# A Mamba-2 scan in front of a cosine router: another order of the scan's steps, with banks of their own for the last outputs

## The chip, the cores and the metric

The kernel runs on one core of one Trainium2 chip. The metric is the device time of one execution in microseconds (us), lower is better. A profiled execution comes with its span (first to last instruction of the core), the granted clock of TensorE and the instructions of all engines: PE (TensorE matmul), PEld (its weight loads), DVE (VectorE), ACT (ScalarE), POOL (GpSimd) and SP (SyncE, which issues loads here).

## What is computed

Two blocks follow each other: a state-space scan over 4 batches, 8 heads and 768 tokens, and a top-1 mixture of 8 experts over the 3072 tokens that come out of it.

```python
for c in range(nc):                       # chunks of 32 tokens, nc = 24
    cum = np.cumsum(la, axis=-1)          # la = log of the decays a
    L = np.exp(cum[:, :, :, None] - cum[:, :, None, :]) * causal
    y_intra = einsum('bhij,bhjd->bhid', einsum('bhin,bhjn->bhij', Cc, Bc) * L, xc)
    y_inter = einsum('bhin,bhnd->bhid', Cc, state) * exp(cum)[..., None]
    y[:, :, sl] = y_intra + y_inter
    state = exp(sum(la))[..., None, None] * state + sum over j of B_j x_j * exp(cum_last - cum_j)
...
logits = xn @ en.T / tau                  # x = y as 3072 tokens of 256
expert_idx = argmax(logits, axis=1)
...
out[mask] = gate_w[mask, None] * (np.maximum(x[mask] @ w1[e], 0.0) @ w2[e])   # for each expert e
```

## The kernel before

The kernel takes chunks of 128 tokens (`Q`), each in two halves of 64 (`HQ`). There are 6 such chunks (`NC`) and 4 batches, and one step of the scan treats a pair of batches of one chunk, so there are 12 pairs (`NP`), two to a chunk. The order of the instructions on every engine is the order in which the Python code calls the functions, and nothing reorders them. Each engine works its own list in order and waits where an operand isn't there.

`begin` (L1358) loads the first data, keeps TensorE busy with products of zeros (L1377, 15 of them with 512 columns), turns the decays into factors and does the parts of pair 0 that need no state. `scan` (L1450) then runs steps s = 1 to 11. A step is made of:

- `inner` (L393, matmuls at L401): the products of C and B of pair s into `pg`. `causal` (L408) masks them on DVE into `g`.
- `from_states` (L427; L437 for the first half with `Tp`, L442 for the second with `Tq`) and `within` (L448; L458): the outputs of pair s-1 from the carried states and from the pair's own tokens, both into the bank pair `py`. `keep_outputs` (L555; L558) copies them on ACT to `yT`.
- `sums` (L465; L473): what pair s adds to the states, into columns 256 to 383 of `pg`. `states` (L480) folds it into the carried states, on ACT, DVE and POOL; `blocks_of_first` and `blocks_of_second` lay them out as `Tq` and `Tp` for `from_states`.
- `finish` (L563; L567): the outputs `yT` of pair s-2 are turned so that tokens lie on partitions, and the logits come with them, into `pz`. `keep_tokens` (L573; L577) copies them on ACT to `yt`, and `keep_rows` (L580) writes them to DRAM by a DMA that ACT issues.
- `scale_x` (POOL, `xs`), `scale_c` (POOL, `cp`) and `split_c` (ACT, `cm`) prepare the next pairs.

The routing of a chunk is spread over the steps: `pick` and `picked` (DVE) find each token's expert, `count` (POOL) counts them, `ranks` (L623; L631, ten small bf16 instructions on PE) numbers them, `hots` and `rows_hot` (DVE, and POOL for `Z`) make one-hot matrices, and `tables` (L680; L683) and `add_table` place the token numbers in a table by expert. `scan_end` (L1526) finishes pair 11 and the last two chunks' routing, while expert job J0, which takes tokens of the first four chunks, starts: a gather of its rows by POOL (`early`, L1605), `turn`, then `plain_up` (L1042) and `plain_down` (L1053). `moe` (L1613) does the rest of the experts.

Loads go through SP's queue in order. The table `LOADS` (L1424) says what is loaded in which of four places of a step; each load waits (`behind`, L338) for the last matmul issued so far.

Of PE's program, one fp32 matmul is two weight loads and two products, so four instructions; one in bf16 is two.

Of the kernel before, what the change touches and what calls it, by code (L numbers as in the profile page):

```python
# [124 lines left out]
def more_route_consts(k):  # L125
    nc = k.nc
    k.before = tile_(k, "before", [128, 128], BF16)
    k.ones = tile_(k, "ones", [128, 128], BF16)
# [297 lines left out]

def from_states(k, p):  # L427
    nc = k.nc
    c, b, t = pair(k, p)
    s = k.un[p]  # L430
    for i in range(2):
        first = c > 0 and i == 0
        a = slice(128 * i, 128 * i + 128)
        if c > 0:
            for g in range(2):
                r = slice(64 * g, 64 * g + 64)
                nc.tensor.matmul(  # L437
                    k.py[r, 0, a], lhsT=k.Tq[2 * c][r, b + i].rearrange("p q d -> p (q d)"),
                    rhs=s.cm[r, i, 0].rearrange("p v s -> p (v s)"), start=first, stop=False,
                    tile_position=(64 * g, 64 * g), skip_group_check=True,  # L440
                )
        k.last = nc.tensor.matmul(  # L442
            k.py[:, 1, a], lhsT=k.Tq[2 * c + 1][:, b + i].rearrange("p q d -> p (q d)"),
            rhs=s.cm[:, i, 1].rearrange("p v s -> p (v s)"), start=first, stop=(c == 0), skip_group_check=True,
# [3 lines left out]
def within(k, p):  # L448
    nc = k.nc
    c, b, t = pair(k, p)  # L450
    s = k.un[p]
    for i in range(2):
        for v in range(2):
            for q in range(4):
                for h in range(2):
# [3 lines left out]
                        k.py[r, h, a : a + HQ], lhsT=s.xs[m, i, n : n + 32], rhs=s.g[m, q, 2 * i + v, :],  # L459
# [5 lines left out]
def sums(k, p):  # L465
# [14 lines left out]
def states(k, p):  # L480
# [21 lines left out]
    if not last:  # L502
# [3 lines left out]
        )  # L506
    blocks_of_first(k, i, bb, u[0])
# [47 lines left out]
def keep_outputs(k, p):  # L555
# [3 lines left out]
        out=s.yT[:].rearrange("p j h s -> p h j s"), in_=k.py[:, :, 0:256].rearrange("p h (j s) -> p h j s", j=4)  # L559
    )  # L560


def finish(k, p):  # L563
    yT = k.un[p].yT
    for i in range(2):
        for j, at in ((0, 0), (1, LG)):
            k.last = k.nc.tensor.matmul(  # L567
                k.pz[:, i, at : at + Y1], lhsT=yT[:, 2 * i + j].rearrange("p h s -> p (h s)"), rhs=k.turn[:, j, :],
# [4 lines left out]
def keep_tokens(k, p):  # L573
# [3 lines left out]
    k.nc.scalar.copy(out=k.yt[c][:, b : b + 2, :], in_=k.pz[:, :, 0:W])  # L577
# [12 lines left out]
def pick(k, c):  # L590
# [9 lines left out]
    n = w.tile(ub, F32, name="nth", tag="nth")  # L600
# [35 lines left out]
def hots(k, c, at):  # L636

    nc = k.nc
    w = k.work
# [15 lines left out]
    k.hot[c] = r, ge  # L655


def rows_hot(k, c):
# [699 lines left out]
def begin(k):  # L1358
# [11 lines left out]
    load(k, 0, ("ct", "bt", "x", "b"))  # L1370
    expert_emb(k)
# [4 lines left out]
    for i in range(15):  # L1376
        nc.tensor.matmul(k.pg[:, 3, :], lhsT=k.zero[:, 0:128], rhs=k.zero[:], start=True, stop=True)  # L1377
    decays(k, 0)
    centre_decays(k, 0)
# [10 lines left out]
    behind(k, load(k, 1, ("ct",)), k.last)  # L1390
    load_decays(k, (4, 5), (nc.sync,))
# [10 lines left out]
    behind(k, load(k, 1, ("bt",)), k.last)  # L1402
# [5 lines left out]
    behind(k, load(k, 1, ("x0",)), k.last)  # L1408
    warm(k, 3)
# [350 lines left out]
```

## Time and profile before

| what | us |
|---|---|
| three runs, median (lowest, highest) | 273.12 (272.39, 273.99) |
| the profiled execution's own time | 271.15 |
| its span, first to last instruction | 269.2 |
| PE busy in the span | 249.0 (92%) |
| DVE, ACT, POOL busy | 172.2, 122.3, 130.4 |
| mean granted clock of TensorE | 0.936 of full |

In the rows of the trace, a time is counted from the span's start. A row of the timeline has the start, the duration, the engine, the line, the tile written and those read, the count, and in brackets the idle time of the engine just before, with what ended it; "issue" means that nothing which the profile shows was waited for. Matmuls of one group overlap, so the distance from one group's start to the next group's is what a group costs, not the duration of its row.

### The profile page before, as it was taken

To read this page: it belongs to the slowest core of one execution; us is meant where nothing else is said; L and a number is where in the kernel's file an instruction comes from. 1 tells how busy PE (TensorE), PEld (TensorE's weight loads), DVE (VectorE), ACT (ScalarE), POOL (GpSimd) and SP (SyncE) were. 2 spreads that over 40 slices of the span, in tenths; PEclk is the share of its full clock that TensorE was granted. 3 is DMA by queue.
4 is the path that set the end of the run, shared out by engine and by line. 5 is a ranking of instruction groups with operands and counts; after the bars stand their busy time and mean duration, and the time that the engine had idled before them with its cause. 6 is when DMAs were issued, how large, how long until landed. Compare 5 with 4: busy or idle time off the path is not lost.

```text
span 269.2 us, 7547 instructions
## 1 busy us (share of the span) xinstructions
PE 249.0 (92%) x2921; PEld 222.7 (83%) x2922; DVE 172.2 (64%) x502; ACT 122.3 (45%) x342; POOL 130.4 (48%) x242
## 2 busy tenths in 40 slices
PE   8879989999888998999999999999999999999790
PEld 2657758787667998999999999999899899899670
DVE  7757763766522480639839869948947957948630
ACT  3354562554212235456337535717626627626520
POOL 8773967466242273830635445455365365305214
PEclk9977995999955799999999999999999999999997
DMA  5586858745412069990534525526525121001001
GB/s 170 171 238 202 273 120 253 230 129 161 136 59 83 1 196 317 376 258 18 189 100 139 184 67 191 172 65 201 173 68 189 29 64 39 20 0 49 11 0 53
DMA packets 22949, 36.32 MB, mean 135 GB/s; under 512 B 2601, under 2 KB 15282, under 8 KB 22912
## 3 DMA queue, kind: packets, MB, share of 16 engines
q1 hardware_dynamic: 16272, 25.78, 30.7%
q0 software_dynamic: 3024, 6.67, 8.8%
q10 hardware_dynamic: 3616, 3.39, 3.7%
q8 instruction: 23, 0.38, 0.6%
q14 instruction: 14, 0.11, 0.1%
HBM read 29.33 MB, written 6.52 MB: 133 GB/s over the span
## 4 chain that ended last, share of the span: by engine, by line
PE 72%; issue 13%; ACT 5%; DMA 3%; POOL 3%; DVE 1%; POOLq 1%; ACTq 0%
PE by L927 10%; PE bx L927 9%; PE bx L987 9%; PE pz L567 6%; PE by L987 5%; PE py L458 4%; DMA out_dram<-yof,s_rest 3%; PE py L442 3%; PE bx L1042 3%; PE pg L401 3%; PE py L437 2%; PE by L1042 2%; PE bx L1053 2%; ACT sqf L863 2%; PE pg L1377 2%
## 5 line engine op out<-in xcount | busy, mean ns | idle before, releaser
L1026 POOL DMA_INDIRECT out_dram<-yof,s_rest x28 | 28.8, 1028 | 46.3 <-ACT yof L1025 45.0
L851 POOL DMA_INDIRECT xgf<-rows,g_rest x28 | 31.9, 1139 | 8.0 <-issue 7.8
L867 POOL TENSOR_TENSOR nrf<-nrf,half 104x4 f32<-104x4 f32 x7 | 7.3, 1041 | 31.0 <-ACT sqf L863 27.3
L567 PE MATMUL pz<-turn,yT 128*128 128x136 f32 x96 | 18.2, 343 | 1.1 <-ACT yt L577 0.6
L411 DVE TENSOR_TENSOR g<-pg,mask 128x1024 f32<-128x1024 f32 x12 | 14.7, 1221 | 4.2 <-PE pg L401 4.0
L567 PEld LDWEIGHTS pz<-turn,yT 128*128 128x128 f32 x96 | 15.6, 238 | 2.0 <-issue 1.0
L558 ACT COPY yT<-py 128x512 f32<-128x512 f32 x12 | 7.0, 583 | 16.5 <-PE py L458 15.0
L577 ACT COPY yt<-pz 128x528 f32<-128x528 f32 x12 | 7.2, 598 | 16.1 <-PE pz L567 16.1
L386 POOL TENSOR_TENSOR xs<-x,rT 128x512 f32<-128x512 f32 x12 | 12.7, 1062 | 3.2 <-DMA x<-in_x_dram 1.5
L524 POOL TENSOR_TENSOR T<-u,whole 128x64 f32<-128x64 f32 x22 | 7.6, 349 | 13.3 <-DVE u L499 12.7
L458 PE MATMUL py<-g,xs 64*32 64x64 f32 x768 | 12.3, 245 | 0.8 <-issue 0.6
L863 ACT ACTIVATE sqf<-xgf 104x256 f32<-104x256 f32 x28 | 11.6, 415 | 1.7 <-DVE h12f L974 1.0
L927 PE MATMUL by<-xsf,w 128*128 128x208 f32 (+6 forms) x56 | 11.8, 333 | 0.6 <-DVE h22f L956 0.6
L442 PE MATMUL py<-cm,Tq 128*128 128x128 f32 x48 | 12.3, 348 | 0.0
L952 DVE TENSOR_TENSOR h12f<-bx,cf 128x416 f32<-128x416 f32 (+6 forms) x7 | 3.9, 555 | 12.9 <-ACT yof L1025 8.6
L401 PE MATMUL pg<-cm,bt 32*64 32x128 f32 x384 | 10.0, 306 | 2.1 <-issue 1.5
L927 PE MATMUL bx<-xsf,w 128*128 128x208 f32 (+6 forms) x56 | 11.7, 331 | 0.0
L458 PEld LDWEIGHTS py<-g,xs 64*32 64x32 f32 x768 | 9.5, 116 | 2.5 <-issue 1.9
L927 PE MATMUL bx<-xsf,s 128*128 128x208 f32 (+6 forms) x56 | 11.4, 326 | 0.0
L927 PE MATMUL by<-xsf,s 128*128 128x208 f32 (+6 forms) x56 | 11.4, 326 | 0.0
L927 PE MATMUL by<-xTf,w 128*128 128x208 f32 (+6 forms) x56 | 11.4, 326 | 0.0
L927 PE MATMUL bx<-xTf,w 128*128 128x208 f32 (+6 forms) x56 | 11.4, 326 | 0.0
(330 smaller groups left out, 702.9 us busy)
## 6 DMA issues: line engine op xcount, KB each, us to landing
w<-in_moe_w_dram SPq DMA_DIRECT2D x14, 1024.0 KB, 4.9
rows<-yt ACTq DMA_DIRECT2D x12, 264.0 KB, 2.2
x<-in_x_dram SPq DMA_DIRECT2D x10, 256.0 KB, 4.2
w<-in_moe_w_dram SPq DMA_DIRECT2D x8, 256.0 KB, 3.1
ct<-in_CT_dram SPq DMA_DIRECT2D x6, 256.0 KB, 2.8
bt<-in_BT_dram SPq DMA_DIRECT2D x6, 256.0 KB
b<-in_B_dram SPq DMA_DIRECT2D x6, 256.0 KB, 5.6
F<-fd SPq DMA_DIRECT2D x4, 260.0 KB
```

The costliest lines, as they stand in the source:

```text
L386: k.nc.gpsimd.tensor_tensor(out=s.xs[:].rearrange("p i (h d) -> p (i h) d", d=D), in0=t.x[:, b : b + 2, :].rearrange("p i (h d) -> p (i h) ...
L401: k.last = nc.tensor.matmul(k.pg[m, q, 128 * i : 128 * i + 128], lhsT=t.bt[r, b + i, m], rhs=s.cm[r, i, h].rearrange("p v s -> p (v s)"), ...
L411: k.nc.vector.tensor_tensor(out=s.g[:], in0=k.pg[:, :, 0:256].rearrange("p q (t i) -> p q t i", t=4), in1=k.mask[:].unsqueeze(1).unsqueeze ...
L442: k.last = nc.tensor.matmul(k.py[:, 1, a], lhsT=k.Tq[2 * c + 1][:, b + i].rearrange("p q d -> p (q d)"), rhs=s.cm[:, i, 1].rearrange("p v ...
L458: k.last = nc.tensor.matmul(k.py[r, h, a : a + HQ], lhsT=s.xs[m, i, n : n + 32], rhs=s.g[m, q, 2 * i + v, :], start=(c == 0 and i == 0 and ...
L567: k.last = k.nc.tensor.matmul(k.pz[:, i, at : at + Y1], lhsT=yT[:, 2 * i + j].rearrange("p h s -> p (h s)"), rhs=k.turn[:, j, :], start=(j ...
L851: k.nc.gpsimd.indirect_dma_start(out=s.x[:, i, 0:W], out_offset=None, in_=k.rows[0:rows, :], in_offset=bass.IndirectOffsetOnAxis(ap=s.g_id ...
L863: nc.scalar.activation(sq[:], s.x[:, i, :].rearrange("p (j w) -> p j w", j=KD)[:, :, 0:128], ACT.Square, accum_out=s.nr[:, i : i + 1],)
L927: s.k.nc.tensor.matmul(bank[:, w * i : w * i + w], lhsT=a[:, 2 * g + i, :], rhs=s.r1[p], start=(p in (1, 2, 5) and i == 0), stop=True, ski ...
L987: s.k.nc.tensor.matmul(bank[:, 0:w], lhsT=a[:, g, :], rhs=r[:, g, 0:w], start=(p in (1, 2, 5) and g == 0), stop=True, skip_group_check=True,)
L1026: d = nc.gpsimd.indirect_dma_start(out=k.out[:, :], out_offset=bass.IndirectOffsetOnAxis(ap=s.s_idx[0:n, i : i + 1], axis=0), in_=y[0:n], ...
L1042: nc.tensor.matmul(bank[:, 0:n], lhsT=s.wt.w1[:, j, 128 * f : 128 * f + 128], rhs=s.xT[:, j, 0:n], start=(j == 0), stop=(j == KD - 1),)
```

## The change

The scan is written in another order. Steps 1 and 2 go to a function of their own, `first_steps`; `scan` runs steps 3 to 11.

- Within a step, `finish` of pair s-2 and its `keep_tokens` stand right behind `inner`, then `ranks`, then `sums` and `states` of pair s; `from_states` and `within` of pair s-1, with `keep_outputs`, come last. Before, `from_states` and `within` stood behind `inner`, and `finish` was last.
- `from_states` does the four blocks of `Tp` for both batches, then the two of `Tq`; before, the two kinds took turns.
- The places of a chunk's tokens are found a step sooner: `ranks` runs at even steps with pair-wise functions split up (`pick1`, `pick2`, `hots1`, `hots2`, `columns_hot`), and `ranks` writes `py` instead of `pz`.
- The outputs of the last pair (11) go to columns of `pg`, and its tokens to `py`; the table of chunk 3 and J0's gather come in step 11, before `causal`.
- The sums of the last chunk leave out the half that no later chunk reads.
- `begin` loads `ct` and `bt` of chunk 1 at once; `LOADS` has three places in a step, not four.
- The products of zeros are 80 with 64 columns in place of 15 with 512, and 8 with 128 columns in place of 3 with 512 ahead of step 1.
- `scan_end`: two DMAs of rows become one, `plain_up` 2 stands ahead of `ranks` of chunk 5, `plain_up` 4 ahead of the last `tables`.

On PE, an odd step with a table (s = 7 in the list after; before, the table stood in even steps, here s = 8). L401 is `inner`, L437 and L442 `from_states`, L458 `within`, L473 `sums`, L683 `tables`, L567 `finish`. Before:

```order
L401 MATMUL pg<-cm,bt 64x128 x16
L437 MATMUL py<-cm,Tp 64x128 x2
L442 MATMUL py<-cm,Tq 128x128
L437 MATMUL py<-cm,Tp 64x128 x2
L442 MATMUL py<-cm,Tq 128x128
L458 MATMUL py<-g,xs 32x64 x32
L473 MATMUL pg<-xs,b 32x64 x16
L683 MATMUL pz<-Z,A 104x32 x4
L567 MATMUL pz<-turn,yT 128x136 x4
```

After; the lines of the changed file are L579 for `finish`, L479 for `sums`, L440 and L446 for `from_states`, L712 for `tables` and L464 for `within`:

```order
L401 MATMUL pg<-cm,bt 64x128 x16
L579 MATMUL pz<-turn,yT 128x136 x4
L479 MATMUL pg<-xs,b 32x64 x16
L440 MATMUL py<-cm,Tp 64x128 x4
L446 MATMUL py<-cm,Tq 128x128 x2
L712 MATMUL pz<-Z,A 104x32 x4
L464 MATMUL py<-g,xs 32x64 x32
```

`finish` moved from the end of the step to the second place, and the two products into `py` from the second place to the end. The outputs that `finish` turns were written by the last group of the step before.

On PE at the end of the scan, before: from the sums of step 11 to `finish` of pair 10 (bx is a bank of the job's pool):

```order
L473 MATMUL pg<-xs,b 32x64 x16
L567 MATMUL pz<-turn,yT 128x136 x4
L683 MATMUL bx_1647<-Z,A 104x32 x4
L437 MATMUL py<-cm,Tp 64x128 x2
L442 MATMUL py<-cm,Tq 128x128
L437 MATMUL py<-cm,Tp 64x128 x2
L442 MATMUL py<-cm,Tq 128x128
L458 MATMUL py<-g,xs 32x64 x32
L567 MATMUL pz<-turn,yT 128x136 x4
```

and after, from `inner` of step 11 to the products of the last pair:

```order
L401 MATMUL pg<-cm,bt 64x128 x16
L712 MATMUL py<-Z,A 104x32 x4
L579 MATMUL pz<-turn,yT 128x136 x4
L440 MATMUL py<-cm,Tp 64x128 x4
L446 MATMUL py<-cm,Tq 128x128 x2
L479 MATMUL pg<-xs,b 32x64 x8
L464 MATMUL py<-g,xs 32x64 x32
L440 MATMUL pg<-cm,Tp 64x128 x4
L446 MATMUL pg<-cm,Tq 128x128 x2
L464 MATMUL pg<-g,xs 32x64 x32
```

The table of chunk 3 moved up right behind `inner` of step 11, the sums have 8 matmuls in place of 16, and the last pair's products go to `pg`.

On ACT, one step, before (L558 `keep_outputs`, L492 a part of `states`, L577 `keep_tokens`, L582 the rows' DMA, L550 `blocks_of_second`, L377 `split_c`):

```order
L558 COPY yT<-py 128x2x4x64
L492 ACTIVATE u<-pg,tmask 128x64
L577 COPY yt<-pz 128x528
L582 DMA rows<-yt 128x2x264
L550 ACTIVATE Tp<-T,pmask 128x2x32 x2
L377 ACTIVATE cm<-cp,tmask 128x4x64 x2
```

and after (L565 `keep_outputs`, L498, L589 `keep_tokens`, L595 the DMA, L557, L377):

```order
L377 ACTIVATE cm<-cp,tmask 128x4x64 x2
L589 COPY yt<-pz 128x528
L498 ACTIVATE u<-pg,tmask 128x64
L557 ACTIVATE Tp<-T,pmask 128x2x32 x2
L565 COPY yT<-py 128x2x4x64
L595 DMA rows<-yt 128x2x264
```

The copy to `yT` is now the last ACT work of a step, and between it and the matmuls that read it stands PE's `inner` alone.

The core of the diff:

```diff
 def begin(k):
...
     load(k, 0, ("ct", "bt", "x", "b"))
+    load(k, 1, ("ct", "bt"))
+    load_decays(k, (4, 5), (nc.sync,))
...
-    for i in range(15):
-        nc.tensor.matmul(k.pg[:, 3, :], lhsT=k.zero[:, 0:128], rhs=k.zero[:], start=True, stop=True)
+    for i in range(80):
+        nc.tensor.matmul(k.pg[:, 3, 0:64], lhsT=k.zero[:], rhs=k.zero[:, 0:64], start=True, stop=True)
...
-    warm(k, 3)
+    warm(k, 8)
...
+def place_out(k, p):
+    return k.pg[:, 2:4, :] if p == NP - 1 else k.py[:]
...
+def place_tokens(k, p):
+    return (k.py if p == NP - 1 else k.pz)[:]
...
 def sums(k, p):
...
-            for h in range(2):
+            for h in range(2 if c < NC - 1 else 1):
...
 LOADS = {
-    4: ["3bt", "4ct", "4x0", ""],
+    4: ["3x0", "3x1", "3bt"],
...
-    at, tab = k.pz[:, 1, 288 : 288 + NB * E], k.pz[0:TR, 0, 288 : 288 + E * NT]
-    for s in range(1, NP):
+    first_steps(k)
+    at, tab = k.py[:, 1, 0 : NB * E], k.py[0:TR, 0, 0 : E * NT]
+    for s in range(3, NP):
+        odd = s % 2
+        picks, ranked, listed = (s - 3) // 2, (s - 4) // 2, (s - 5) // 2
+        end = s == NP - 1
         inner(k, s)
+        if end:
+            tables(k, listed, tab)
+            add_table(k, listed, tab)
+            early(k)
         causal(k, s)
         transfers(k, s, 0)
...
+        finish(k, s - 2)
+        transfers(k, s, 1)
+        keep_tokens(k, s - 2)
...
+        if not odd:
+            ranks(k, ranked, at)
+            hots1(k, ranked, at)
+        if end:
+            from_states(k, s - 1)
+            transfers(k, s, 2)
+        sums(k, s)
...
+        states(k, s, lambda: odd or (hots2(k, ranked), s == 10 and rows_hot(k, ranked)))
...
+        if not end:
+            from_states(k, s - 1)
+            transfers(k, s, 2)
+        if odd and not end and listed >= 0:
+            tables(k, listed, late[0:TR, 0 : E * NT])
+            add_table(k, listed, late[0:TR, 0 : E * NT])
+        within(k, s - 1)
+        keep_outputs(k, s - 1)
+        keep_rows(k, s - 2)
+    outputs(k, NP - 1)
+    keep_outputs(k, NP - 1)
+    ranks(k, 4, at)
...
```

More of the change, by code (lines that the diff above doesn't have):

```diff
@@ L477, in sums, with states @@
                 )
-def states(k, p):
+def states(k, p, between=lambda: None):
     nc = k.nc
@@ L1401, in begin @@
     inner(k, 0)
-    behind(k, load(k, 1, ("bt",)), k.last)
+    behind(k, load(k, 1, ("x0",)), k.last)
     scale_x(k, 0)
@@ L1407, in begin @@
     sums(k, 0)
-    behind(k, load(k, 1, ("x0",)), k.last)
-    warm(k, 3)
+    behind(k, load(k, 1, ("x1",)), k.last)
+    warm(k, 8)
     causal(k, 0)
@@ L1463, in scan @@
             split_c(k, s + 1)
-        if new is not None:
-            pick(k, new)
-        if s == 1:
-            scale_emb(k)
-        if s == 2:
-            decays(k, 1)
-        if s == 3:
-            inverse(k, 1)
-            more_route_consts(k)
-        if s == 2:
-            turn_emb(k)
-        outputs(k, s - 1, lambda: known is not None and ranks(k, known, at))
-        keep_outputs(k, s - 1)
-        if known is not None:
-            hots(k, known, at)
-        transfers(k, s, 1)
-        sums(k, s)
-        transfers(k, s, 2)
         if s == 4:
@@ L1520, in scan @@
[L1520 to L1523 removed]
+        blocks_of_second(k, s - 2)
+        if odd:
+            if end:
+                pick1(k, picks)
+            pick2(k, picks)
+            count(k, picks)
+        if s == 3:
+            inverse(k, 1)
+        if not end:
+            from_states(k, s - 1)
+            transfers(k, s, 2)
+        if odd and not end and listed >= 0:
+            tables(k, listed, late[0:TR, 0 : E * NT])
+            add_table(k, listed, late[0:TR, 0 : E * NT])
@@ new lines, in scan, with first_steps @@
+        within(k, s - 1)
[4 more added lines that the diff above has]
+    ranks(k, 4, at)
+    hots1(k, 4, at)
+    hots2(k, 4)
+    columns_hot(k, 4)
+    rows_hot(k, 4)
+    finish(k, NP - 2)
+    keep_tokens(k, NP - 2)
+def first_steps(k):
+    for s in (1, 2):
+        inner(k, s)
+        causal(k, s)
+        transfers(k, s, 0)
+        split_c(k, s + 1)
+        if s == 1:
+            scale_emb(k)
+            nc = k.nc
+            k.ones = tile_(k, "ones", [128, 128], BF16)
+            nc.vector.memset(k.ones[:], 1.0)
+            k.sums = tile_(k, "sums", [128, NC + 1, E], BF16)
+            nc.vector.memset(k.sums[:, 0, :], 0.0)
+        within(k, s - 1)
+        if s == 2:
+            turn_emb(k)
+        from_states(k, s - 1)
+        keep_outputs(k, s - 1)
+        transfers(k, s, 1)
+        sums(k, s)
+        transfers(k, s, 2)
+        if s == 2:
+            decays(k, 1)
+            inside(k, 1)
+        scale_x(k, s + 1)
+        scale_c(k, s + 2)
+        states(k, s)
+        if s == 2:
+            run_decays(k, 1)
+            blocks_of_second(k, 0)
+            more_route_consts(k)
+            finish(k, 0)
+            keep_tokens(k, 0)
+            keep_rows(k, 0)
@@ L1551, in scan_end @@
     J.keep_turned(1, b1)
-    pick(k, 5)
-    picked(k, 5)
-    count(k, 5)
+    finish(k, NP - 1)
+    keep_tokens(k, NP - 1)
+    keep_rows(k, NP - 2, 2)
     X = [b2, b0, b1]
     J.plain_up(0, X[0])
+    pick1(k, 5)
+    pick2(k, 5)
+    count(k, 5)
     tables(k, 4, tab)
@@ L1587, in scan_end @@
     load_weights(k, 2)
-    for f in range(4, 6):
-        J.plain_up(f, X[f % 3])
+    J.plain_up(5, X[2])
     k.J0.squares()
```

190 lines of the change are left out of this document (86 added, 104 removed).

## The prediction

> **What bounds the kernel now.** I start with the page and the list of DMA queues.
>
> ```profile
> PE 249.0 (92%) x2921; PEld 222.7 (83%) x2922; DVE 172.2 (64%) x502; ACT 122.3 (45%) x342; POOL 130.4 (48%) x242
> PEclk9977995999955799999999999999999999999997
> q8 instruction: 23, 0.38, 0.6%
> ```
>
> PE is the busy engine, so time is to be had only where it idles or where its clock is granted at half. The clock row has three dips in its first half, during the scan. A table by stretches puts edges on them (columns: length, busy time of each engine, granted clock, DMA share, GB/s):
>
> ```profile
> 16.30:23.10 6.80, 6.67 (x144) 5.50 (x146) 4.40 (x16) 2.89 (x9) 4.68 (x11) 0.50 0.80 227
> 23.10:40.20 17.10, 15.72 (x464) 11.83 (x462) 12.55 (x31) 9.81 (x27) 11.77 (x31) 1.00 0.70 198
> 40.20:47.00 6.80, 6.80 (x150) 5.67 (x148) 2.39 (x9) 1.87 (x5) 5.04 (x11) 0.50 0.84 254
> 74.30:91.40 17.10, 15.44 (x126) 13.20 (x127) 4.97 (x25) 3.38 (x8) 5.66 (x14) 0.50 0.16 51
> ```
>
> I call them A, B and C. At half clock, half the busy time is lost: 6.67/2 = 3.3, 6.80/2 = 3.4 and 15.44/2 = 7.7 us. A and B are 6.8 long and C is 17.1, which is 2 and 5 times 3.4; the starts lie 7 and 10 times 3.4 apart. So the clock is set at ticks of about 3.4 us, and not below two ticks. PE's timeline shows what stands ahead of each:
>
> ```profile
> 13.27 0.41 PE L473 MATMUL pz<-xs,b 64*32 64x64 f32 x20
> 15.12 0.33 PE L473 MATMUL pz<-xs,b 64*32 64x64 f32 x12 [1.44 <-issue]
> 36.62 0.69 PE L401 MATMUL pg<-cm,bt 32*64 32x128 f32 x30
> 38.42 0.37 PE L401 MATMUL pg<-cm,bt 32*64 32x128 f32 x2 [1.12 <-issue]
> 72.96 0.92 PE L683 MATMUL bx<-Z,A 128*104 128x32 f32 x8 [0.78 <-POOL Z L673]
> 77.66 0.52 PE L458 MATMUL py<-g,xs 64*32 64x64 f32 x13 [0.32 <-issue]
> 80.97 2.18 PE L567 MATMUL pz<-turn,yT 128*128 128x136 f32 x8 [0.57 <-ACT yt L577]
> 84.61 1.76 PE L1042 MATMUL bx<-xTh,w 128*128 128x208 f32 x4 [0.76 <-ACT xTh L905]
> 103.17 1.32 PE L1042 MATMUL by<-xTh,w 128*128 128x208 f32 x6 [0.76 <-ACT xTh L905]
> ```
>
> The tick of 16.3 follows a gap of 1.44, that of 40.2 one of 1.12, that of 74.3 one of 0.78 with the end of another of 0.56 (below). The gap of 0.76 at 103.17 is followed by no dip. I conclude that about 1.1 us of idle PE in one 3.4 us stretch halves the clock and 0.76 doesn't; and that C lasts long because gaps go on inside it.
>
> [...]
>
> Two gaps stand inside a group, after 20 of 32 and after 30 of 32 matmuls with the same operands, so no operand was missing. Step 11 shows what was:
>
> ```profile
> 66.03 0.65 PE L401 MATMUL pg<-cm,bt 32*64 32x128 f32 x19
> 67.08 0.47 PE L401 MATMUL pg<-cm,bt 32*64 32x128 f32 x13 [0.41 <-issue]
> 67.48 0.44 PE L437 MATMUL py<-cm,Tp 64*64 64x128 f32 x4
> 67.85 0.49 PE L442 MATMUL py<-cm,Tq 128*128 128x128 f32 x2
> 68.27 0.43 PE L437 MATMUL py<-cm,Tp 64*64 64x128 f32 x4
> 68.63 0.49 PE L442 MATMUL py<-cm,Tq 128*128 128x128 f32 x2
> 68.96 0.18 PE L631 MATMUL pz<-ob,before 128*128 128x32 bf16 x1
> 68.99 0.18 PE L631 MATMUL pz<-sums,ones 128*128 128x32 bf16 x1
> 69.01 0.22 PE L631 MATMUL pz<-ob,ones 128*128 128x24 bf16 x3
> 69.16 0.86 PE L458 MATMUL py<-g,xs 64*32 64x64 f32 x64
> 69.82 0.51 PE L473 MATMUL pg<-xs,b 64*32 64x64 f32 x32
> 70.26 0.38 PE L567 MATMUL pz<-turn,yT 128*128 128x136 f32 x1
> 71.20 0.97 PE L567 MATMUL pz<-turn,yT 128*128 128x136 f32 x7 [0.56 <-issue]
> ```
>
> From the gap's end at 67.08 to the next gap stand 13+4+2+4+2+1+1+3+64+32+1 = 127 matmuls, with as many weight loads 254 instructions. The q8 row moves 0.38 MB in 23 packets, 16.5 KB each, 65 bytes for each of 254; and 23 times 254 is 5842, as many as PE and PEld have instructions in the page's first row (2921 + 2922). So PE's program comes in blocks of some 254 instructions, and a gap is a block that came late. Counting by groups from 15.12 puts 38.42 exactly five blocks on. When a block has begun, the next is there 71.20 - 67.08 = 4.1 us later, an estimate of mine for the others too. At full clock PE can eat a block in less: groups with small tiles take 0.62 (L401), 0.66 (L458) and 0.44 (L473) for 64, 128 and 64 instructions, and those with few cost 1.48 for 24 (L437 and L442, 67.48 to 68.96). **Which groups fall into a block therefore decides whether PE starves.**
>
> [...]
>
> **The change part by part.** The sum is made against the profiled execution's own 271.15 us (span 269.2); the median of the runs shown is 273.12, so I add the same difference to the median.
>
> *Opening, -1.0.*
>
> ```profile
> 5.50 0.15 DVE L188 TENSOR_TENSOR f<-at,w 128x2 f32<-128x2 f32 x1
> 1.24 5.77 PE L1377 MATMUL pg<-zero 128*128 128x512 bf16 x15 [1.24 <-DVE zero L60]
> 6.94 0.37 PE L235 MATMUL pz<-f,spread 32*128 32x130 f32 x1
> ```
>
> The factors were ready at 5.65, but PE spent until 6.94 on zeros, with no idle. 80 products of 64 columns are 5120 columns for 7680, so 2/3 of 5.7 = 3.8 us, if weight loads hide; pairs in L631 with 32 columns follow each other by 0.02 to 0.04. I take 5.9 as the new start of L235. If each pair took 0.10, it would end at 9.2: +2.3. Bounds -1.3 and +2.3. `ct` and `bt` of chunk 1 move to the front, behind pair 0's loads, so they delay none of these; decays 4 and 5 move with them.
>
> *Stretch A, 0.* The first block that was late ended at PE's 442nd instruction (20 of 32 of L473 in step 1). 130 more instructions in the first zeros and 10 in the second put the same count into `within` of step 1, after 36 of 128, with the block before it now asked for during the zeros. The next block holds the rest of `within` (0.47), `from_states` (for chunk 0 only L442, 0.42 for two from 67.85 to 68.27, so 0.84), `sums` 0.44, `inner` 0.62 and 26 of `within` 0.13: 2.5 us against 4.1. So a gap of up to 1.6 only moves from step 1 to step 2, and A stays. If PE waits for operands there anyway, A goes: bounds -4.7 (1.44 + 3.3) and 0.
>
> *Stretch B, -4.0.* Its block now ends elsewhere. Every 254 instructions from the 442nd, I walk through the new list: blocks that hold `from_states` (1.48) and `finish`, and often a table, last about 4 us or more. The poorest in steps 3 to 10 runs from `within` of step 5 (96 of 128 left, 0.50) over `inner` 0.62, `finish` and `ranks` to `sums` 0.44 of step 6.
>
> ```profile
> 64.17 0.92 PE L683 MATMUL pz<-Z,A 128*104 128x32 f32 x8
> 64.92 1.17 PE L567 MATMUL pz<-turn,yT 128*128 128x136 f32 x8
> 70.05 0.58 ACT L558 COPY yT<-py 128x512 f32<-128x512 f32 x1 [2.29 <-PE py L458]
> ```
>
> `tables` cost 64.92 - 64.17 = 0.75, `finish` 66.03 - 64.92 = 1.11, `ranks` 0.20 (68.96 to 69.16). [...] B's 1.12 + 3.4 go, 0.5 comes: -4.0. Bounds -4.5 and 0. The three loads of a step come later in it: `bt` of chunk 3 is asked for behind `from_states` of step 4 and needed at `inner` of step 6, about 0.66 + 5 us later.
>
> ```profile
> b<-in_B_dram SPq DMA_DIRECT2D x6, 256.0 KB, 5.6
> ```
>
> The slowest such load takes 5.6 us in the median, so this is nearly hidden; I take 0, at most +0.5 at steps 6, 8 and 10. The rows' DMA moves behind the copy of `yT` on ACT; what queues behind it is `split_c`, needed only a step later.
>
> *The new wait, +2.1.* `finish` now needs `yT`, which ACT copies from the last `within`. By the rows, ACT starts 0.23 after the group behind `within` (70.05 - 69.82) and takes 0.58, so 0.81; `inner` covers 0.62. PE waits 0.2, and as its weight load waits with it, 0.3, at steps 4 to 10 (in step 3 and 11 other groups lie between): 7 x 0.3. Behind it on PE stand `ranks`, `sums` and both products, and DVE's states wait for the sums. Bounds 0 and 7 x 0.6 = 4.2.
>
> *Less work, -0.8.* Two steps have half of `sums`: 2 x 0.22. [...]
>
> *Stretch C and its gaps, -10.7.* The table that PE awaited at 72.96 is now made in step 10 and 11, where `from_states` and `within` lie behind it; `finish` of pair 11, which waited 0.57 for the bank of pair 10's copy, has `py`; the copies of 84.61 run under `finish`. So 0.56 + 0.78 + 0.32 + 0.57 + 0.76 = 3.0 go, and 7.7 of half clock.
>
> *A new stretch at the end, +4.3.* [...] Bounds 0 and +4.8.
>
> *The last table, +0.5.*
>
> ```profile
> 89.15 1.73 PE L1042 MATMUL bx<-xTh,w 128*128 128x208 f32 x4
> 90.69 0.82 POOL L673 TENSOR_TENSOR Z<-ob,o 128x128 f32<-128x128 bf16 x1
> ```
>
> Chunk 5's `ranks` end at 89.15, `Z` at 91.51: 2.4 us. Under it lay a `plain_up` at half clock; now two at full clock, 1.5 us: PE waits up to 0.9, I take 0.5.
>
> Behind that, gathers, weights and jobs keep their order, and PE has hardly a gap, so it all moves up. Sum: -1.0 + 0 - 4.0 + 2.1 - 0.8 - 10.7 + 4.3 + 0.5 = -9.6. That is 261.5 beside 271.15, and **263.5** beside the median.
>
> **The rivals.**
>
> 1. The forecast: two dips of two ticks, A and the one at the end. 260 to 266.5 us. Chance 0.40.
> 2. Blocks come in time: the gap at the end is below what halves the clock (-4.3), or A goes as well (-4.7): 259.2 and 254.5. For it: blocks are asked for ahead; against it: the short blocks counted above. 0.27.
> 3. One dip more, or C in part: a `bt` or a block delayed by loads adds its gap to the wait for `yT`: +3.4 to +5, 266.9 to 268.5. For it: DMA share is 0.70 to 0.84 in the scan. 0.15.
> 4. Slower: the wait for `yT` and a late block meet in most 3.4 us stretches. If `finish` waits 0.75, not 0.3, a stretch with a late block passes 1.1, the clock dips for two ticks, recovers for one and dips again: in 35 us of steps 4 to 10, 35/10.2 = 3.4 dips of 3.4, +11.6 us: 275.1. It decides from 0.75 per step on. Against it: ACT is free when `within` ends. 0.12.
> 5. The dips don't come from gaps and stay, lengths and all. Then only gaps and work count: -1.0 - 1.1 + 0.5 + 2.1 - 0.8 - 3.0 + 0.95 + 0.5 = -1.9, less the zeros' doubt of about 1: 272 to 271. Against it: three dips, each behind gaps of 1.1 us or more, and none elsewhere. 0.06.
>
> **How the numbers follow.** A measurement of this kernel can tell about 0.5% (1.4 us) from no change. Cases 1 to 3 are faster by more: 0.82. Case 5 is within it: 0.06. Case 4 is slower: 0.12. The range reaches from case 2 with one dip fewer and some of A's gap gone, 256, to the upper part of case 3 with the zeros' bound, 270.5; it leaves out the lowest end of case 2, case 4 and case 5.
>
> **What would show it.** Right: L235 starts near 5.9; step 11's `inner` starts 3 to 8 us before 66.03; `plain_up` starts near 73 to 75, not 84.61, and the last half-clock stretch is at most 7 us. A gap of 1 us or more inside a group in step 2, and one ahead of the last `ranks`, would confirm the blocks. `finish` idles 0.2 to 0.4 behind ACT's `yT` in steps 4 to 10; if it idles 0.75 or more, case 4 is on. If the dips keep their lengths with no gaps ahead of them, my reading of the clock is wrong. The prediction fails if `plain_up` starts after 80.

## The result, and the profile after

The changed kernel takes 261.88 us in the median of 4 runs (261.39 to 262.43), the kernel before 272.75 (271.25 to 273.99): a ratio of 0.960, 95% interval 0.955 to 0.966. The forecast was 263.5. The profiled execution took 261.39, its span is 259.3. In the table of runs below, medians are over all executions, while the ratios leave out those more than 1.5% above the fastest of their kernel, of which the kernel before has many. From the page:

```profile
PE 235.0 (91%) x2960; PEld 216.2 (83%) x2960; DVE 173.4 (67%) x502; ACT 122.1 (47%) x342; POOL 130.3 (50%) x242
PEclk9689999999999999999999999999999999999996
q8 instruction: 24, 0.39, 0.7%
```

One dip of the scan is left in the clock row, in the opening; A, B and C are gone. The table by stretches says where the time came from. Before, cut at step 2's `inner`, step 11's `inner` and the first matmul of the main jobs:

```profile
15.38:66.03 50.65, 48.60 (x1378) 38.54 (x1369) 33.32 (x94) 25.18 (x67) 33.90 (x83) 0.87 0.68 202
66.03:115.36 49.33, 44.95 (x431) 40.40 (x431) 21.73 (x96) 15.03 (x45) 22.21 (x36) 0.83 0.53 169
115.36:269.20 153.84, 143.53 (x893) 137.36 (x892) 106.61 (x273) 76.67 (x216) 63.80 (x87) 0.99 0.32 98
```

and after, cut at the same three matmuls:

```profile
15.63:67.46 51.83, 42.62 (x1366) 34.48 (x1358) 34.79 (x98) 25.36 (x68) 33.34 (x86) 1.00 0.61 187
67.46:105.53 38.07, 36.63 (x415) 33.94 (x410) 20.62 (x91) 14.78 (x45) 21.00 (x32) 1.00 0.68 218
105.53:259.30 153.77, 143.52 (x893) 137.36 (x892) 106.62 (x273) 76.78 (x216) 63.95 (x87) 0.98 0.33 101
```

**All of the gain lies from the start of step 11 on**: 38.07 for 49.33, -11.26. The opening is 0.25 longer, and steps 2 to 10, the part that the change rewrites most, are 1.18 longer although their clock went from 0.87 to full. PE was busy for 42.62 of 51.83 there, where it had been for 48.60 of 50.65: it now idles. PE's timeline shows where:

```profile
20.39 0.69 PE L401 MATMUL pg<-cm,bt 32*64 32x128 f32 x31 [0.45 <-DVE u L510]
21.88 0.32 PE L401 MATMUL pg<-cm,bt 32*64 32x128 f32 x1 [0.81 <-issue]
26.01 0.45 PE L401 MATMUL pg<-cm,bt 32*64 32x128 f32 x10
27.39 0.66 PE L401 MATMUL pg<-cm,bt 32*64 32x128 f32 x22 [0.92 <-issue]
31.06 0.71 PE L464 MATMUL py<-g,xs 64*32 64x64 f32 x46
33.82 0.38 PE L464 MATMUL py<-g,xs 64*32 64x64 f32 x18 [2.05 <-issue]
50.96 0.45 PE L401 MATMUL pg<-cm,bt 32*64 32x128 f32 x8 [0.79 <-issue]
54.41 0.84 PE L464 MATMUL py<-g,xs 64*32 64x64 f32 x62
57.52 0.27 PE L464 MATMUL py<-g,xs 64*32 64x64 f32 x2 [2.27 <-issue]
```

Five gaps inside groups, 6.84 us together, where the kernel before had 1.43 in the same steps (1.12 and 0.31). Yet none of them halved the clock. So two things needed explaining: why gaps of 2.05 and 2.27 are harmless here when 1.12 was not before, and what the end gained if not only clock.

### The profile page after: what moved, and what is told of

The parts are those of the page before. It is cut to its first block, busy times and chain, and to the rows that moved or that the text cites. A ratio compares the mean times of both kernels' runs of the same rounds, so it can differ in the third digit from the quotient of the medians.

```text
span 259.3 us, 7621 instructions
## 1 busy us (share of the span) xinstructions
PE 235.0 (91%) x2960; PEld 216.2 (83%) x2960; DVE 173.4 (67%) x502; ACT 122.1 (47%) x342; POOL 130.3 (50%) x242
## 4 chain that ended last, share of the span: by engine, by line
PE 66%; issue 14%; DMA 7%; ACT 4%; DVE 4%; POOL 3%; POOLq 1%; DVEq 0%
PE by L956 11%; PE bx L956 10%; PE bx L1016 9%; PE by L1016 5%; PE py L464 4%; DMA out_dram<-yof,s_rest 4%; PE pg L401 3%; PE py L446 3%; PE pz L579 2%; DMA x<-in_x_dram 2%; DVE g L411 2%; PE bx L1082 2%; ACT sqf L892 2%; PE by L1082 2%; PE by L1071 2%
## 5 line engine op out<-in xcount | busy, mean ns | idle before, releaser
L565 ACT COPY yT<-py 128x512 f32<-128x512 f32 x11 | 6.4, 586 | 21.3 <-PE py L464 18.0
L464 PE MATMUL py<-g,xs 64*32 64x64 f32 x704 | 10.9, 232 | 4.9 <-issue 4.9
L531 POOL TENSOR_TENSOR T<-u,whole 128x64 f32<-128x64 f32 x22 | 8.3, 380 | 12.2 <-DVE u L505 11.3
L464 PEld LDWEIGHTS py<-g,xs 64*32 64x32 f32 x704 | 8.4, 109 | 6.8 <-issue 5.9
L579 PE MATMUL pz<-turn,yT 128*128 128x136 f32 x88 | 13.0, 290 | 0.2
L401 PE MATMUL pg<-cm,bt 32*64 32x128 f32 x384 | 9.9, 294 | 3.4 <-issue 2.5
L579 PEld LDWEIGHTS pz<-turn,yT 128*128 128x128 f32 x88 | 10.9, 190 | 1.6 <-ACT yT L565 1.2
L981 DVE TENSOR_TENSOR h12f<-by,cf 128x416 f32<-128x416 f32 (+6 forms) x7 | 3.9, 554 | 11.6 <-ACT yof L1054 7.5
L589 ACT COPY yt<-pz 128x528 f32<-128x528 f32 x11 | 6.6, 599 | 10.2 <-PE pz L579 8.2
```

What stands on the lines that cost most here:

```text
L401: k.last = nc.tensor.matmul(k.pg[m, q, 128 * i : 128 * i + 128], lhsT=t.bt[r, b + i, m], rhs=s.cm[r, i, h].rearrange("p v s -> p (v s)"), ...
L464: k.last = nc.tensor.matmul(o[r, h, a : a + HQ], lhsT=s.xs[m, i, n : n + 32], rhs=s.g[m, q, 2 * i + v, :], start=(c == 0 and i == 0 and v ...
L531: k.nc.gpsimd.tensor_tensor(out=k.T[i + 1][:, bb, :], in0=u[:], in1=k.whole[:, i, bb].unsqueeze(2).to_broadcast([128, 2, D]), op=ALU.mult,)
L579: k.last = k.nc.tensor.matmul(o[:, i, at : at + Y1], lhsT=yT[:, 2 * i + j].rearrange("p h s -> p (h s)"), rhs=k.turn[:, j, :], start=(j == ...
```

## The experiments

My theory was the forecast's: PE's program comes in blocks, and a window with about 1.1 us of idle PE halves the clock. Its rivals: the clock goes by the rows that PE is fed, not by idle time; the end gained by waits taken away and not by clock; gaps come from loads alone. Chips differ (the kernel before had medians of 269.17, 270.85 and 266.36 us on the three chips of the table), so each run is read beside the kernel before on its own chip.

| run | us, median (range) | before beside it | ratio, 95% |
|---|---|---|---|
| zeros only | 267.17 (262.55-277.58) | 269.17 (265.12-273.17) | 0.978-0.994 |
| fill, 128 rows | 261.89 (259.57-263.80) | same | 0.968-0.986 |
| fill, 32 rows | 261.88 (259.11-262.24) | same | 0.971-0.985 |
| zeros at the end | 265.67 (263.72-269.83) | same | 0.986-0.996 |
| after, again | 262.35 (261.78-264.64) | 270.85 (267.39-273.88) | 0.969-0.979 |
| loads late | 260.78 (258.96-261.69) | same | 0.962-0.972 |
| opening's loads | 263.27 (261.62-263.68, one 577) | same | 0.969-0.980 |
| old banks | 264.01 (262.64-266.92) | same | 0.973-0.984 |
| rows by chunk | 260.27 (259.85-261.32) | 266.36 (263.32-270.16, one 1291) | 0.982-0.989 |
| loads late, again | 262.31 (259.29-264.74) | same | 0.978-0.992 |
| late table | 264.81 (261.05-269.30) | 265.97 (261.57-271.04, one 465) | 0.992-1.006 |

**The changed kernel again**, with no edit.

> The changed kernel, on the chip of this call and beside the runs that follow. By blocks that end at fixed instructions, the gaps stand at the same places as in the first run (step 3's inner after 31 of 32, step 4's after 10, step 4's outputs after 46 of 64, step 8's after 62 of 64) and only their lengths differ; if the gaps came from transfers alone, their places would move too. 260 to 264 us.

The gaps stood at the same instructions (step 3 after 31 of 32, step 4 after 46 of 64, step 8 after 24 of 32 and 62 of 64), with other lengths. The one in step 4's `inner` after 10 of 32 did not come; one in step 2 and one in the last pair's `within`, which the first execution did not have, did. The gain stood at the end again:

```profile
67.31:106.53 39.22, 36.76 (x412) 33.93 (x409) 20.34 (x90) 14.74 (x45) 20.67 (x32) 1.00 0.66 208
```

That is 39.22 for 49.33; the opening took 12.78 for 15.38, and steps 2 to 10 took 54.53 for 50.65. Here is the gap of step 4, and PE's table for two windows of the clock:

```profile
29.05 0.71 PE L464 MATMUL py<-g,xs 64*32 64x64 f32 x46
31.77 0.38 PE L464 MATMUL py<-g,xs 64*32 64x64 f32 x18 [2.01 <-issue]
```

```profile
28.84:32.25 3.41, 1.40 (x77) 1.02 (x83) 2.24 (x6) 0.77 (x4) 2.79 (x6) 1.00 0.91 321
32.25:35.66 3.41, 3.41 (x71) 2.83 (x66) 2.24 (x2) 1.62 (x4) 2.60 (x6) 0.50 0.59 172
```

The same gap in the first execution of the changed kernel, with the ticks of that execution:

```profile
29.19:32.60 3.41, 2.58 (x97) 1.97 (x96) 2.21 (x10) 1.56 (x5) 2.26 (x5) 1.00 0.97 325
32.60:36.01 3.41, 2.19 (x59) 1.80 (x58) 1.35 (x2) 1.39 (x3) 3.17 (x7) 1.00 0.51 158
```

A gap of 2.0 lies inside one window in the one execution (1.40 busy, 2.0 idle) and the clock is halved; in the other a tick cuts it at 32.60 into 0.83 and 1.22, and the clock stays. That is why the gaps of 2.05 and 2.27 were harmless: where the ticks fall, and they fall anew in each execution. I cut the fourteen traces of this case at their ticks, up to 245 us, and counted PE's idle time in each window that ran at full clock:

| idle in the window, us | windows | clock halved behind |
|---|---|---|
| under 0.9 | 850 | 0 |
| 0.9 to 1.5 | 57 | 4 |
| 1.51 and more | 22 | 22 |

and in each window at half clock that begins behind the first 6 us:

| idle in the window, us | windows | clock stayed at half |
|---|---|---|
| none (under 0.03) | 28 | 2 |
| 0.03 to 0.2 | 6 | 4 |
| 0.2 and more | 14 | 14 |

**In these traces the clock halved each time behind 1.51 us of idle or more in one window (22 of 22), and it came back almost only behind a window with next to none (26 of 28 with under 0.03 us, 2 of 20 with more).** In the first 6 us that was looser: four windows with 0.21 to 0.41 us of idle were followed by full clock, four with 0.21 to 0.83 were not. Waits far too short to cause a stretch (none of 850 windows with under 0.9 us did) kept it going. That is C: its windows held 0.32, 0.57, 0.72 and 0.04 us of idle. The stretches in the run above were one tick long, not the two that I had taken for the least.

**Zeros at the end**, in the kernel before:

```diff
+    hold(k, b2, 3)
     tables(k, 3, tab)
...
+    hold(k, b2, 2)
     finish(k, NP - 2)
...
+    hold(k, b2, 3)
     J.plain_up(0, X[0])
```

> The kernel before with 8 products of zeros (128 rows, 512 columns, 0.2 us each) at the end of the scan where PE waits: 3 ahead of the table at 72.96, 2 ahead of the outputs of pair 10, 3 ahead of the job's first products. Order and waits stay. If stretch C is a matter of the clock alone and its 7.7 us are lost to half clock, it goes: 272.7 - 7.7 + 0.5 = 265.5 us (264.5 to 267). If the change gained there by taking waits away and the clock is a side effect, 272 to 273. If rows or idle time in later windows bring a stretch of two ticks back: 268 to 269.

3.5 us less in the median and 2.4 by the ratio (0.991), for the expected 7; the kernel before was itself at 269.2 on this chip, not at 272.7. The clock did what was asked; the table for the end, and what PE waited for in it:

```profile
66.32:110.99 44.67, 40.23 (x438) 35.32 (x438) 21.90 (x96) 15.03 (x45) 22.21 (x36) 1.00 0.58 185
```

```profile
PE bx L683 <- POOL Z L673: 1.3, 2, 0.7
PE pg L401 <- issue: 0.8, 1, 0.8
PE by L1042 <- ACT xTh L905: 0.6, 1, 0.6
PE pz L567 <- ACT yt L577: 0.6, 1, 0.6
PE bx L1042 <- ACT xTh L905: 0.4, 1, 0.4
PE py L458 <- issue: 0.4, 1, 0.4
```

Full clock all through, and 44.67 for 49.33: the clock alone is worth 4.7 between these two executions, while the change gets 38.07. What the changed kernel still waits for there:

```profile
PE py L464 <- issue: 0.6, 2, 0.4
PE bx L1633 <- DVE oh L652: 0.3, 1, 0.3
PE bx L1043 <- ACT yTh L1087: 0.2, 1, 0.2
PE bx L1082 <- ACT hTh L1075: 0.2, 1, 0.2
```

Of the other 6.6, waits are 4.1 in the first rows and 1.7 that the eight zeros filled (two of them took 0.44, 77.87 to 78.31), less the 1.3 that stay: 4.5. The rest is PE's busy time, 40.23 less the zeros for 36.63. At half clock one of these waits had been hidden behind slow matmuls: the last table waited for nothing before and 0.63 for `Z` here. So clock and waits can't be priced quite one by one. By this count the rival holds for a good part: the waits, 4.5, are worth as much as the clock, 4.7, and 2 is less work on PE.

**Old banks**, in the changed kernel:

```diff
-    return k.pg[:, 2:4, :] if p == NP - 1 else k.py[:]
+    return k.py[:]
...
-    return (k.py if p == NP - 1 else k.pz)[:]
+    return k.pz[:]
```

> The changed kernel with the outputs of pair 11 in the bank of all others and its tokens in theirs, as before the change. Three waits come back: the last outputs for the copy of pair 10's (0.8), the last ranks for the copy of pair 11's (0.8), the turn of pair 11's for the copy of pair 10's tokens (0.4 to 0.6): 2.0 us more, and 1.6 of them in one window of 3.4 us. With a clock that halves at 1.5 us of idle in a window, a stretch of two ticks or more comes with them, 3.4 us: 5.4 more than the changed kernel. If the clock stays, 2.0 more. If the order of the steps alone had made the gain, no difference.

264.01 for 262.35, +1.66, with ranges that overlap. The trace shows the waits that came:

```profile
PE py L440 <- ACT yT L565: 0.7, 1, 0.7
PE py L643 <- ACT yT L565: 0.7, 1, 0.7
PE pz L579 <- ACT yt L589: 0.3, 1, 0.3
```

1.7, and no half clock at the end: no window held more than 1.25 us of idle there. The end took 39.98 for 38.07 in the first execution of the changed kernel. The banks of their own are worth these three waits.

**Late table**: table and gather of step 11 where they stood before.

```diff
         inner(k, s)
-        if end:
-            tables(k, listed, tab)
-            add_table(k, listed, tab)
-            early(k)
...
+    tables(k, 3, late[0:TR, 0 : E * NT])
     outputs(k, NP - 1)
     keep_outputs(k, NP - 1)
+    add_table(k, 3, late[0:TR, 0 : E * NT])
+    early(k)
```

> The changed kernel with the table of chunk 3 and the job's gather moved back: from right behind inner of step 11 to where they stood before, ahead of the last pair's products and behind the copy of its outputs. PE's work is the same. In the changed kernel the gather's two transfers are issued from 70.2 to 72.7 and the turn of its rows starts at 76.7 with no wait. Moved, the table is ready 5 us later, the gather is issued from about 75 to 77.5 and its rows are there at 79 to 80: PE waits 2 to 3 us ahead of the job's turn, and a stretch of half clock of one or two ticks may follow: 2 to 3 us more than the changed kernel without a stretch, 4 to 6 with one. If the gather has slack, no difference.

```profile
77.29 0.28 PE L927 MATMUL bx<-ident,xgh 104*128 104x104 f32 x1 [1.86 <-DMA xgh<-rows,g_early]
78.93 0.49 PE L927 MATMUL bx<-ident,xgh 104*128 104x104 f32 x3 [1.36 <-DMA xgh<-rows,g_early]
```

PE waits 3.2 for the gather, a stretch of half clock follows, one window long (the mean clock of the end is 0.96), and the end takes 41.90 (67.03 to 108.93) for 38.07. On this chip that left no difference from the kernel before that can be told (0.992 to 1.006); the changed kernel itself was not run on it. Of the pieces of the end that were tried alone, this is the largest.

**Fill, with 128 and with 32 rows**, in the changed kernel's opening:

```diff
-    for i in range(80):
+    for i in range(58):
...
+    fill(k, 10)
     inner(k, 0)
...
+    fill(k, 12)
```

> The changed kernel with 22 products of zeros (128 rows, 128 columns) in the opening's two idle places, 10 ahead of the first inner product and 12 behind it, and 58 zeros of 88 columns in place of 80 of 64 ahead, so that as many instructions stand before the scan. By idle time and by rows alike the window from 5.3 to 8.7 us is now used (idle 0.91 to about 0.3; rows 0.47 to about 0.65 of full), the half-clock stretch from 8.7 to 15.5 goes and 2 to 3 us with it: 259 to 260 us beside 261.9.

> As the run with 22 products of zeros, but each uses 32 of PE's 128 rows, with the same columns, count and places. If idle time sets the clock, the stretch from 8.7 to 15.5 goes as with 128 rows: 259 to 260 us. If the rows fed set it (0.47 to about 0.52 of full in that window), it stays: 261.5 to 262.5 us.

Times are the same, neither is at the 259 to 260 expected, and no opening was halved in either. The window that decides, with 32 rows, and the one behind it:

```profile
5.05:8.47 3.42, 3.06 (x67) 2.51 (x65) 2.99 (x9) 0.66 (x4) 2.70 (x12) 1.00 0.94 333
8.47:11.88 3.41, 2.90 (x117) 2.11 (x103) 2.38 (x6) 1.69 (x5) 3.25 (x8) 1.00 0.68 178
```

0.36 idle, and full clock behind it. By my count of columns times rows in the traces, the first of these windows was fed 1.1 times what the window that was halved in the first execution was (0.53 for 0.47 on the scale of the expectation), and two others with 0.85 times as much (0.40: zeros only, and the opening's loads) were not halved. The theory of rows falls. Idle time doesn't single out that window either: it held 0.91 us, and those two 0.92. The fill bought nothing, since the changed kernel run again had no stretch in its opening either.

**The opening's loads as before**:

```diff
-    load(k, 1, ("ct", "bt"))
-    load_decays(k, (4, 5), (nc.sync,))
...
     turn_inverse(k, 0, r)
+    behind(k, load(k, 1, ("ct",)), k.last)
+    load_decays(k, (4, 5), (nc.sync,))
...
-    behind(k, load(k, 1, ("x0",)), k.last)
+    behind(k, load(k, 1, ("bt", "x0")), k.last)
```

> The changed kernel with the opening's loads as before: ct of chunk 1 behind the factors' turn, decays 4 and 5 there too, bt and x0 of chunk 1 behind the first inner product. If the transfers brought forward hold up x of chunk 0, for which sums of step 0 waited 1.63 us, that wait goes and step 1's inner starts 1 to 1.6 us sooner: 0.5 to 1.6 us less than the changed kernel. If x is late for another reason, no difference.

No difference. In the first execution of the changed kernel `sums` waited 1.63 for POOL's `xs`, which waited for the transfer of `x`, and step 1 began late; in the second it didn't (one fence for each):

```profile
10.13 0.68 PE L479 MATMUL pz<-xs,b 64*32 64x64 f32 x32 [1.63 <-POOL xs L386]
11.71 1.15 PE L401 MATMUL pg<-cm,bt 32*64 32x128 f32 x32
```

```profile
8.83 0.46 PE L479 MATMUL pz<-xs,b 64*32 64x64 f32 x32 [0.34 <-POOL xs L386]
9.94 0.70 PE L401 MATMUL pg<-cm,bt 32*64 32x128 f32 x32
```

So the wait doesn't come in every execution. It came in two more of those with the change's loads (2.46 in the run without the loads of chunks 3 to 5, 1.64 with the late table), in none of the other seven, and with the old loads too (1.01 in the run with zeros only). So a late `x` doesn't need the loads that the change moved forward.

**Zeros only**, in the kernel before:

```diff
-    for i in range(15):
-        nc.tensor.matmul(k.pg[:, 3, :], lhsT=k.zero[:, 0:128], rhs=k.zero[:], start=True, stop=True)
+    for i in range(80):
+        nc.tensor.matmul(k.pg[:, 3, 0:64], lhsT=k.zero[:, 0:128], rhs=k.zero[:, 0:64], start=True, stop=True)
...
-    warm(k, 3)
+    warm(k, 8)
...
-            k.py[:, 0, :], lhsT=k.zero[:, 0:128], rhs=k.zero[:], start=True, stop=True, skip_group_check=True
+            k.py[:, 0, 0:128], lhsT=k.zero[:, 0:128], rhs=k.zero[:, 0:128], start=True, stop=True, skip_group_check=True
```

> The kernel before with the new zeros alone (80 of 64 columns, then 8 of 128), 140 more of PE's instructions ahead of the scan. The forecast's theory (blocks, and a clock that halves behind about 1.1 us of idle): L235 starts at 5.9, -1.0; the blocks' ends move by 140 instructions, so the gaps of 1.44 and 1.12 stand elsewhere, and each stretch A and B stays or goes with its gap: 266 to 272 us. Theory of rows (the clock follows how many of PE's rows are fed in a window of 3.4 us, not the idle time): the 16 matmuls of L235 with 32 of 128 rows now stand alone in a window and put a half-clock stretch into the opening, as after the change; A goes or stays by what its window holds: 269 to 273 us. If the zeros are most of the change's gain: 262 to 265 us. The stretch C stays by all three, 17 us.

2.0 less, with a range of 15 us, so the zeros may bring a part of the gain, and not the most of it. With 140 more instructions ahead, the blocks' ends fall elsewhere and the gaps with them. The gap of step 1's sums is gone; there is one of 1.38 in step 2's `within`, after 11 of 64, and this one in the sums of step 4:

```profile
28.50 0.48 PE L473 MATMUL pg<-xs,b 64*32 64x64 f32 x29
32.27 0.42 PE L473 MATMUL pg<-xs,b 64*32 64x64 f32 x3 [3.29 <-issue]
```

Stretches like A and B were there in other steps, 3.4 and 10.2 us long, and C in its old place, 17.1.

**Loads late**, in the changed kernel:

```diff
-    3: ["2b", "", "3F 3ct"],
-    4: ["3x0", "3x1", "3bt"],
+    3: ["2b 3F", "3ct", ""],
+    4: ["", "", "3x0 3x1 3bt"],
...
-    8: ["5x0", "5x1", "5bt"],
+    8: ["", "", "5x0 5x1 5bt"],
```

> The changed kernel with three groups of loads moved: the decays and ct of chunk 3 a place or two sooner, x and bt of chunk 3 from step 4's first two places to its end, x and bt of chunk 5 likewise in step 8. If it is the transfers under way that hold up the fetch of an instruction block (it began 4.0 and 3.5 us after the block before had begun, against 1.0 to 1.6 where the queues were idle), the gaps of 2.05 and 2.27 in steps 4 and 8 shrink to 0.7 or less: 3 us less than the changed kernel beside it. If the fetch goes by its own pace, they stay and the time is the same within 1 us.

The two gaps shrank to 1.50 and 1.17 (2.01 and 1.72 in the changed kernel beside it), not to 0.7, and the time by 1.6, with ranges that just do not meet. So I took the loads away:

```diff
+        if what[0] in "345":
+            c = int(what[0])
+            k.ld[c] = k.ld[c - 3]
+            if c == 3:
+                k.ld[c].f = k.ld[1].f
+            continue
```

> The changed kernel without the loads of chunks 3, 4 and 5 (x, b, bt, ct, decays): their steps compute with the data of chunks 0, 1 and 2, so the results are other ones, with the same instructions on PE at the same places. If the loads under way are what holds up the fetch of a block, it begins 1.0 to 1.6 us after the block before has begun, and the gaps of step 4 (2.0), step 8's inner (0.9) and step 8's outputs (1.7 to 2.3) shrink to 0.4 or less; 3 to 5 us less than the changed kernel's 262, 257 to 259. If the fetch goes by its own pace or waits for the rows that ACT writes, the gaps stay at 0.6 to 2 and the time at 260 to 262.

With other data the tokens go to other experts, and the whole takes 516 us; only the scan is read.

```profile
26.70 0.66 PE L401 MATMUL pg<-cm,bt 32*64 32x128 f32 x22 [0.66 <-issue]
30.38 0.71 PE L464 MATMUL py<-g,xs 64*32 64x64 f32 x46
32.32 0.38 PE L464 MATMUL py<-g,xs 64*32 64x64 f32 x18 [1.24 <-issue]
54.33 0.21 PE L464 MATMUL py<-g,xs 64*32 64x64 f32 x1 [0.91 <-issue]
```

Still 1.24 and 0.91, against 2.0 and 1.7 to 2.3 with loads. Neither theory has it all: about half of each gap goes with the loads, and half is there without any. Ahead of these two gaps, the next block's transfer began 2.9 us after the block had begun (26.70 to 29.62; 49.10 to 51.99), by the instruction packets of the trace; in the other blocks of the scan it began 0.1 to 3.0 us after. What sets that pace stays open.

**Rows by chunk**, the kernel with late loads and the scan's rows written once per chunk, and **loads late, again**:

```diff
-        keep_rows(k, s - 2)
+        if s == 3:
+            keep_rows(k, 1)
+        elif odd:
+            keep_rows(k, s - 3, 2)
```

> The kernel with the loads of chunks 3 and 5 moved, and the rows of the scan written once per chunk (528 KB, behind the odd steps) in place of twice. If the rows' transfers hold up the fetch of blocks too, the gaps in the even steps shrink and those in step 5, 7 or 9 may grow: 259 to 260.5 us beside 260.8. If not, 260.8 as without.

> The changed kernel with the loads of chunks 3 and 5 moved, a second time and on another day of the chip: the blocks' gaps at the same instructions as before, each 0.3 to 1.9 long, and 259 to 262 us. The clock is halved behind each window of 3.4 us that holds 1.5 us of idle PE or more, and behind none with less than 0.9.

260.27 for 262.31 beside it in the median, in a range of 1.5 us, but both have the ratio 0.985: that fewer transfers help is not shown. Gaps of 2.29, 1.34, 1.23, 1.15, 0.90 and 0.74 remain at the old places, 7.7 us. None of them halved the clock: the one of 2.29 was cut by a tick into about 1.1 and 1.2.

Its median is the lowest of the table, but the changed kernel did not run on that chip, so the distance is not measured. In the repeat of the loads alone the gaps were 0.90 to 1.80 long, the one in step 4's `within` did not come, and the two windows with over 1.5 us of idle (1.74 and 1.72) were the two that halved the clock, as expected. `inner` of step 6 waited 1.3 for `bt`, which that edit brings later.

## Why the prediction came out right

The time was right (263.5 forecast, 261.88 measured); of its steps about half were.

By stage, forecast and measured against 271.15: opening -1.0, +0.25; steps 2 to 10 -2.4 (A 0, B -4.0, wait +2.1, most of the work -0.5), +1.18; end -6.2 (C and gaps -10.7, the new stretch +4.3, the last table +0.5, -0.3 of work), -11.26. Sum -9.6, -9.83 (and -0.07 in the main jobs). **Errors of 3.6 us too little in steps 2 to 10 and 5.1 too much at the end cancelled, with 1.2 in the opening: that the sum is so near is luck.** Of my own signs, `plain_up` was to start at 73 to 75 and step 11 three to eight us sooner; they came at 78.05 and 1.4 later.

- *Opening.* Right in size: L235 starts at 5.71 (5.9 forecast), and in the second execution step 1's `inner` at 9.94 for 11.22. One late `x` hid it in the first; in three later runs a clock at half until 13.5 to 13.9 us did (step 1's `inner` at 11.71).
- *A.* The place was right: a gap after 13 of 64 in step 2's `within`, 1.06 in the second execution and 1.72 with the opening's loads as before. The first execution had none there; it came late from the opening, where its half clock lay instead. But in no run of the changed order did a half-clock stretch follow right behind that gap, so the 3.3 us of clock that the forecast left in place went.
- *B.* Wrong. The step that failed: "When a block has begun, the next is there 4.1 us later, an estimate of mine for the others too." It was 6.43 (27.39 to 33.82) and 6.56 (50.96 to 57.52). The transfer itself took about 1 us there; it began only 4.04 and 4.24 us after the block had begun, and 2.9 with the loads taken away. So the poorest blocks were in steps 3, 4 and 8, not in step 6. No run shows the 0.5 that the sum has for a gap in step 6: no run of the changed order had a gap of 0.15 us or more put down to "issue" there, and in the first execution the other steps had 6.84 us. In these runs one block that came late cost up to 3.29 us (the run with zeros only).
- *The wait for `yT`.* Too high. In weight loads it is 0.3 at the most:

```profile
PEld pz L579 <- ACT yT L565: 1.2, 4, 0.3
```

  Four waits and 1.2 for my seven and 2.1; case 4 needed 0.75 in each.
- *Less work.* No run shows the 0.36 that the forecast's 0.8 has beside the 2 x 0.22 of the sums. What the rows show in its place: `from_states` cost 1.22 (29.84 to 31.06) for 1.48, but `within` 0.79 (38.59 to 39.38) for 0.66; a step without a table took 4.52 before (56.36 to 60.88) and after (39.38 to 43.90).
- *C.* The sum was right and its parts weren't: 7.7 of clock and 3.0 of waits were 4.7 and 4.5, with 2 of work besides. I read waits out of a stretch at half clock, where slow matmuls can hide them (0.63 for `Z`, in the run with zeros at the end).
- *The end.* +4.3 forecast, nothing in the first execution. The place was right: a block ends three matmuls ahead of the last `ranks`. The next block came in time in the first execution, and late in the second and in the repeat of the late loads (one row each):

```profile
76.34 0.30 PE L464 MATMUL pg<-g,xs 64*32 64x64 f32 x3 [1.02 <-issue]
```

```profile
74.32 0.42 PE L464 MATMUL pg<-g,xs 64*32 64x64 f32 x3 [1.80 <-issue]
```

  No run shows where the 0.95 us of gap in the forecast's +4.3 comes from; the runs showed none, 1.02 and 1.80 in its place. Of the two only the 1.80 halved the clock. That the first execution had neither gap nor stretch is luck. My limit for the clock was too low, too: "about 1.1 us of idle PE in one 3.4 us stretch halves the clock" is 1.51 each time, and a rare chance from 0.9 (4 of 57).
- *The last table.* 0.28, at the counts behind it, for 0.5.

Case 2 (blocks in time) would have given 259.2 with the end's stretch gone, and in the first execution the end did go its way; the blocks of steps 2 to 10 went the other.

What stays open: why C began behind only 1.08 us of idle, B behind 1.12 and the opening's stretch behind 0.91, where 53 windows with 0.9 to 1.5 did nothing; why B went on behind a window with no idle at all; and the pace of the blocks. The new order within steps 3 to 10 was not run without the rest, so nothing shows that it gains anything.

## What to carry to other kernels

Cut a trace at the ticks of its own clock and count the idle time per window. Here a gap was dear or free by where the tick fell (2.01 us inside one window halved the clock, 2.05 cut into 0.83 and 1.22 did not), so look at more than one execution before you price it. Small waits counted at half clock (behind none of 14 windows with 0.2 us or more did the clock come back), and one did not show its full length there (the last table's 0.63 for `Z`). Where PE runs hundreds of tiny matmuls, count its program between gaps: here 78 of 88 stood at multiples of 256 records, which gave the places where gaps can come, but not their lengths.

## What the hardware showed that I had not expected

- The clock's way back is narrower than its way down: halved behind 1.51 us of idle in a window of 3.41, restored behind the first 6 us only by a window with next to none (26 of 28 restored; 0 of 14 with 0.2 us or more).
- On one chip the kernel before took 263.3 to 264.9 in six executions (mean clock 0.965 to 0.985) and 267.8 to 270.2 in five (0.944 to 0.952). The changed kernel's six of the second set lie within 2.9, those of the kernel before on the same chip (eleven) within 6.5. The ratio was 0.960 in the first set and 0.974 in the second. So a good part of what the change gains in the median is probably stretches of half clock that the old order met more often.
- Gaps stand at one count of instructions, to the matmul, while their lengths vary down to none: the one in step 8 after 62 of 64 was 0.18 long in one run and 2.54 in another. The first 85 us of the fourteen traces have 88 gaps of 0.2 us or more that are put down to "issue". By the count of PE's records, 78 of them lie at multiples of 256 from each other, to one record; the other ten lie in the last two `within`.
